# Linear attention and two MLPs on one core: two operand sums change engine, the next x operands change time, four results change buffer

## The chip, the cores and the metric

One core of one Trainium2 chip runs the whole program. The metric is device time in microseconds (us), the median of several executions; lower is better. One more execution was recorded by the hardware profiler, and every duration below is from that one. Engines are called as the profile calls them: PE is TensorE (its weight loads are PEld), DVE is VectorE, ACT is ScalarE, POOL is GpSimd, SP is the queue of SyncE, which issues nearly all DMAs.

## The reference

```python
q_s = softmax(q, over the head dimension);  k_s = softmax(k, over the sequence)
kv = einsum('bhsd,bhse->bhde', k_s, v);     attn = einsum('bhsd,bhde->bhse', q_s, kv)
x = attn as (4608 tokens, 512)
h = x @ w_in;   x = (h * clip(h + 3, 0, 6) / 6) @ w_out        # first MLP, 512 -> 2048 -> 512
h = x @ w2_in;  out = (h * sigmoid(h)) @ w2_out                # second MLP, same sizes
```

Everything is float32.

## The kernel before

**Number format.** PE multiplies in fp32r, a shorter float32. Each operand is split into a rounded upper part (ACT, a cast) and the rest, the lower part (DVE, a subtraction); a product takes three matmuls, upper by upper, upper by lower and lower by upper.

**First MLP (phase 0).** Tokens go in 9 blocks of 512 (j = 0 to 8) with 16 steps f of 128 hidden units each. A step is `mm1` (L486, 12 matmuls), `gate` (L543) and `mm2` (L552, 12 matmuls into four PSUM banks y0 to y3). After the 16th step `finish` (L567) scales the four banks by 1/6 into tiles `o` and stores them to `yd` in DRAM; DVE takes the even ones, ACT the odd ones. The tiles come from the pool `tmp`, tag `t2k`, which has six buffers and serves most short-lived tiles of the kernel. In the same phase the second MLP's weights are converted, summed and stored to `ws` (class `Parts`, L173); the tile they are stored from has the tag `sp` (one buffer). A tile of tag `qT` (one buffer) serves the attention.

**Second MLP (`second_mlp`, L961).** Blocks 1 to 8 are taken in four pairs (b = 0 to 3). For each pair the two products are done by a scheme that needs seven products P1 to P7 of half-size blocks instead of eight, with sums of blocks as operands and sums of the results afterwards. Block 0 is done last, in the plain way. One pair has two stages, both cut into slots of six matmuls (128x512):

- The inner stage, the first product: 8 groups n of seven slots (`inner`, L983). Behind each group come sums on DVE and one on POOL, sigmoids on ACT, multiplications on DVE that leave the gated values in four half tiles of g (`pair_events`, L1010), and on POOL `t1` and `t2` (L1048, L1051), which make two more operands of the second product: T1, in place, and T2, in the tile `spare`.
- The outer stage, the second product: seven products in the order P1, P5, P6, P2, P7, P3, P4, eight slots i each (`outer`, L1137). Before each slot its operand is split, upper on ACT (`split`, L1079) and lower on DVE (`split_low`, L1083), into one of five tile pairs taken in turn (`split_tile`, L1066). P7 and P4 need two more sums: `next_t3(i)` (L1087) overwrites g1[:, 0], which P1 has used, with T3, and `next_t4(i)` (L1091) overwrites g1[:, 1], which P5 has used, with T4. Both run on POOL. `joins` (L1151) adds the results.

During the inner stages of pairs 0 to 2, `x_ahead` (L1096) makes the operands of the pair after: twice (c = 0 and 1) it loads four tiles from `yd`, makes four sums on POOL (`total`), splits seven operands (`high` on ACT L1109, `low` on DVE L1113) and stores fourteen tiles to `xd`. The outer stage then fetches those (`x_fetch`). The weights arrive through a ring of six buffers (`fetch`, L876).

**Order.** Nothing is reordered by a compiler: every engine works through its own queue in program order. In the second MLP that order is a list of events, `when(t, fn)`, sorted by t, and t is counted in slots: a pair begins at t0, `start[0] = t0 + 55` is the first outer slot, and an event at t stands between the matmuls of slot t and the next. LOOK = 4 puts a split about four slots ahead of its matmuls:

```python
when(t - LOOK + 0.2, lambda b=b, p=p, i=i: split(b, p, i))
when(t - LOOK + 0.5, lambda b=b, p=p, i=i: split_low(b, p, i))
```

The last step of the first MLP is placed at `when(1.95, ...)`, behind the first two slots of pair 0: `mm2(last)` and `finish(0, 8)`.

Of the kernel before, what the change touches and what calls it, by code (L numbers as in the profile page):

```python
# [9 lines left out]
F32 = mybir.dt.float32  # L10
F32R = mybir.dt.float32r
AF = mybir.ActivationFunctionType
ALU = mybir.AluOpType
# [5 lines left out]
P = 128  # L19
# [4 lines left out]
def f32(ap):  # L24
    return ap.bitcast(F32)
# [3 lines left out]
def efficient_attention_then_two_mlps(  # L29
# [11 lines left out]
    nc = tc.nc  # L41
# [6 lines left out]
    NB = NT // BLK  # L48
# [9 lines left out]
    tmp = ctx.enter_context(tc.tile_pool(name="tmp", bufs=6))  # L58
    raw = ctx.enter_context(tc.tile_pool(name="raw", bufs=2))
    gs = ctx.enter_context(tc.tile_pool(name="gs", bufs=2))  # L60
    att = ctx.enter_context(tc.tile_pool(name="att", bufs=1))
# [100 lines left out]
    def slot(o, i, part):  # L162
        if part == "A21":
            return 7 * NPR + i
        if o:
            return OUTER.index(part) * NPR + i
        if part == "A22":
            return 6 + 7 * i + 2 if i < NPR - 1 else 7 * NPR - 1
        return (0 if i == 0 else 6 + 7 * (i - 1)) + INNER.index(part) + (
            1 if i and part not in INNER[:2] else 0  # L170
        )
# [394 lines left out]

    def finish(ph, j):  # L567
        for c, y in enumerate(acc.pop((ph, j))):
            o = tmp.tile([P, 512], F32, tag="t2k", name="o")
            if ph == 0:  # L570
                if c % 2:
                    nc.scalar.mul(o, y, 1.0 / 6.0)
                else:
                    nc.vector.tensor_scalar_mul(o, y, 1.0 / 6.0)
                nc.sync.dma_start(yd[j, c], o)
            else:
                (nc.scalar.copy if c % 2 else nc.vector.tensor_copy)(o, y)
                rows = out[j * BLK : (j + 1) * BLK, :].rearrange("(p i) d -> i p d", i=NCH)
                nc.sync.dma_start(rows[c], o)
# [37 lines left out]
    for i, u in enumerate(range(2, NP)):  # L617
        o = i * (KB + VB + QB)
# [240 lines left out]
    ring, op, gw, ev = [], {}, {}, []  # L859
    LOOK = 4  # L860

    def when(t, fn):
        ev.append((t, len(ev), fn))
# [97 lines left out]
    def second_mlp(last):  # L961
# [16 lines left out]
        def add(out, a, b, how=ALU.add, eng=None):  # L978
            (eng or nc.vector).tensor_tensor(out=out, in0=a, in1=b, op=how)  # L979
# [18 lines left out]
        def g_of(f):  # L998
            if f not in gw:
                gw[f] = wts.tile([P, 2, BLK], F32, tag="wo", name="g2")  # L1000
            return gw[f]
# [64 lines left out]
        def split_tile(x=False):  # L1066
            n = 2 + turns[0] % 3 if x else turns[0] % 5
            turns[0] += 1
            if n == 4:
                return [  # L1070
                    att.tile([P, BLK], F32R, tag=tag, bufs=1, name="gsp") for tag in ("ke", "qe")
                ]
            if n < 2:
                t = gs.tile([P, 2, BLK], F32R, tag="g", name="gsp")
            else:
                t = att.tile([P, 2, BLK], F32R, tag=("sp", "qT")[n - 2], bufs=1, name="gsp")
            return [t[:, 0], t[:, 1]]

        def split(b, p, i):  # L1079
            t = d["sp", b, p, i] = split_tile()  # L1080
            nc.scalar.copy(t[0], source(p, i))  # L1081

        def split_low(b, p, i):  # L1083
            t = d["sp", b, p, i]
            add(t[1], source(p, i), f32(t[0]), ALU.subtract)

        def next_t3(i):  # L1087
            g1 = g_of(2 * i)
            add(g1[:, 0], op["spare"][:, i], g1[:, 0], ALU.subtract, nc.gpsimd)

        def next_t4(i):  # L1091
            add(g_of(2 * i)[:, 1], g_of(2 * i + 1)[:, 0], op["spare"][:, i], ALU.subtract, nc.gpsimd)

        XS = ("B11", "T2", "T1", "B21", "T3", "B22", "T4")

        def x_ahead(j, c, t, step):  # L1096

            st, hl = {}, {}

            def load(n):  # L1100
                if n in ("B22", "B21"):
                    pair = gs.tile([P, 2, BLK], F32, tag="g", name="xst")
                    st[n], st[{"B22": "B12", "B21": "B11"}[n]] = pair[:, 0], pair[:, 1]
                jj, h = j + (n[2] == "2"), int(n[1] == "2")
                nc.sync.dma_start(st[n], yd[jj, 2 * h + c])

            def high(n, src):
                hl[n] = split_tile(True)
                nc.scalar.copy(hl[n][0], st[src])  # L1109

            def low(n, src):
                hi, lo = hl.pop(n)
                add(lo, st[src], f32(hi), ALU.subtract)  # L1113
                to = xd[XS.index(n)]
                nc.sync.dma_start(to[:, 0, c], f32(hi))
                nc.sync.dma_start(to[:, 1, c], f32(lo))

            def total(to, x, y):
                add(st[to], st[x], st[y], ALU.subtract, nc.gpsimd)

            for m, n in enumerate(("B22", "B12", "B21", "B11")):
                when(t - 4.0 + 0.3 * m, lambda n=n: load(n))
            for m, (n, src) in enumerate((
                ("B22", "B22"), ("B21", "B21"), ("T1", "B12"), ("T2", "B22"), ("B11", "B11"),
                ("T4", "B21"), ("T3", "B11"),
            )):
                when(t + m * step + 0.3, lambda n=n, src=src: high(n, src))
                when(t + m * step + 0.9, lambda n=n, src=src: low(n, src))
            when(t + 0.02, lambda: total("B12", "B12", "B11"))
            when(t + 1 * step + 0.25, lambda: total("B22", "B22", "B12"))  # L1130
            when(t + 3 * step + 0.25, lambda: total("B21", "B21", "B22"))
            when(t + 4 * step + 1.0, lambda: total("B11", "B22", "B11"))
# [63 lines left out]
        for b in range(BB):  # L1196
            t0 = T
            place = {}
            for n in range(NPR):
                at = place[n] = {}  # L1200
                for p in ("P1", "P6"):
                    at[p], T = T, T + 1
                if n:
                    place[n - 1]["P4"], T = T, T + 1
                for p in ("P5", "P2", "P7", "P3"):
                    at[p], T = T, T + 1
            t2 = T
            start = {}
            for u in range(7 * NPR):
                start[u], T = T, T + 1  # L1210
                if u == 0:
                    place[NPR - 1]["P4"], T = T, T + 1
            for n in range(NPR):
                pair_events(b, n, place[n])
                for p, t in place[n].items():
                    k = 7 * NPR * b + slot(0, n, PAIR[p][0]) // 2
                    uses[k] = max(uses.get(k, 0.0), t)
            for u in range(7 * NPR):
                p, i = KEYS[u // NPR], u % NPR
                t = start[u]  # L1220
                when(t - LOOK + 0.2, lambda b=b, p=p, i=i: split(b, p, i))
                when(t - LOOK + 0.5, lambda b=b, p=p, i=i: split_low(b, p, i))
                if p == "P1":
                    when(start[0] + 6.4 + 3.0 * i, lambda i=i: next_t3(i))
                if p == "P6":
                    when(start[0] + 26.4 + 2.8 * i, lambda i=i: next_t4(i))
                when(t, lambda b=b, p=p, i=i: outer(b, p, i))
                k = 7 * NPR * b + 7 * NPR // 2 + u // 2
                uses[k] = max(uses.get(k, 0.0), t)
                if i == NPR - 1:  # L1230
                    joins(b, p, t + 1.3)
            j = 1 + 2 * b
            if b + 1 < BB:
                x_ahead(j + 2, 0, t0 + 9.0, 3.2)
                x_ahead(j + 2, 1, t0 + 31.0, 3.2)
                for m, n in enumerate(XS):
                    for low in range(2):
                        when(
                            start[0] + 3.1 + 6.0 * m + 3.0 * low,
                            lambda n=n, low=low: x_fetch(n, low),  # L1240
                        )
                for k in range(2 * NCH):
                    when(T + 3.95 + 5.0 * k, lambda j=j, k=k: turn(j, k))
            else:
                def begin_last():
                    op.pop("spare")
                base = start[0]
                for c in range(NC):
                    when(base + 44.3 + c, lambda c=c: load_y(0, c))
                    when(base + 48.4 + 2 * c, lambda c=c: split_y(0, c))  # L1250
                for f in range(NF):
                    when(base + (4.2 + 2.2 * f if f < 14 else 100.0), lambda f=f: load_split(f, 0))
                for f in range(0, NF, 2):
                    when(base + 48.3 + 0.5 * f, lambda f=f: load_split(f, 1))
# [24 lines left out]
    with tc.manual_schedule(engines=None):  # L1279
# [34 lines left out]
        for n, s in list(enumerate(steps))[NF:]:  # L1314
            ph, j, f = s
# [123 lines left out]
```

## Time and profile before

| | us |
|---|---|
| median of 3 runs (lowest, highest) | 1645.51 (1644.49, 1646.26) |
| the profiled execution | 1645.06 |
| its span, first to last instruction | 1643.3 |
| PE / DVE / ACT / POOL busy in the span | 1611.2 / 1082.1 / 748.6 / 422.4 |
| second MLP, four pairs | from about 899 to 1548 |

The profile's time is split by engine, by line and by stretch. Instructions that run through the helper `add` (L978) all carry line 979, so they are told apart by the names of their tiles: `gsp` is a split tile, `g` a gated tile, `xst` a loaded x tile, `pb` a PSUM bank. A timeline row gives start, length, engine, line, operation and tiles, a count where rows of one kind are merged, and in brackets the idle time of the engine just before and what ended it.

### The profile page before, as it was taken

To read this page: it belongs to the slowest core of one execution; us is meant where nothing else is said; L and a number is where in the kernel's file an instruction comes from. 1 tells how busy PE (TensorE), PEld (TensorE's weight loads), DVE (VectorE), ACT (ScalarE), POOL (GpSimd) and SP (SyncE) were. 2 spreads that over 40 slices of the span, in tenths; PEclk is the share of its full clock that TensorE was granted. 3 is DMA by queue.
4 is the path that set the end of the run, shared out by engine and by line. 5 is a ranking of instruction groups with operands and counts; after the bars stand their busy time and mean duration, and the time that the engine had idled before them with its cause. 6 is when DMAs were issued, how large, how long until landed. Compare 5 with 4: busy or idle time off the path is not lost.

```text
span 1643.3 us, 21988 instructions
## 1 busy us (share of the span) xinstructions
PE 1611.2 (98%) x7612; PEld 1301.1 (79%) x7612; DVE 1082.1 (66%) x1721; ACT 748.6 (46%) x1322; POOL 422.4 (26%) x334
## 2 busy tenths in 40 slices
PE   6999999999999999999999999999999999999998
PEld 4777888888888888888888787887788878887887
DVE  8996666666666666655555689567956885578522
ACT  6885444444434444443434454344435543444322
POOL 2100111111111111111121456055705560345000
PEclk9999999999999999999999999999999999999999
DMA  9912435454543445343341998798879986669730
GB/s 270 325 35 68 133 107 141 124 151 119 170 136 110 140 120 151 110 135 103 113 157 58 334 327 298 250 316 307 301 254 314 342 291 246 216 226 330 251 128 26
DMA packets 291838, 317.61 MB, mean 193 GB/s; under 512 B 113424, under 2 KB 197392, under 8 KB 291728
## 3 DMA queue, kind: packets, MB, share of 16 engines
q1 hardware_dynamic: 228768, 300.97, 54.5%
q10 hardware_dynamic: 62960, 15.25, 4.1%
q8 instruction: 60, 0.98, 0.2%
q14 instruction: 50, 0.41, 0.1%
HBM read 234.62 MB, written 81.53 MB: 192 GB/s over the span
## 4 chain that ended last, share of the span: by engine, by line
PE 84%; DVE 11%; DMA 2%; ACT 2%; issue 1%; POOL 1%; SPq 0%; ACTq 0%; DVEq 0%; POOLq 0%
PE h L493 25%; PE y L563 22%; PE pb L992 16%; PE pb L1145 13%; DVE gsp L979 5%; PE y L565 3%; PE pa L451 2%; PE pa L337 1%; DVE fa L132 1%; DVE fa L128 1%; PE pb L1185 1%; DMA ring<-ws 1%; DMA xd<-gsp 0%; DMA xst<-yd 0%; DVE fa L121 0%
## 5 line engine op out<-in xcount | busy, mean ns | idle before, releaser
L493 PE MATMUL h<-x,wi 128*128 128x512 f32 x1920 | 472.6, 394 | 2.3 <-DVE wi L153 1.0
L493 PEld LDWEIGHTS h<-x,wi 128*128 128x128 f32 x1920 | 356.5, 188 | 78.7 <-DVE wi L153 2.4
L563 PE MATMUL y<-g,wo 128*128 128x512 f32 x1728 | 418.1, 391 | 0.0
L563 PEld LDWEIGHTS y<-g,wo 128*128 128x128 f32 x1728 | 322.4, 188 | 68.1
L1145 PE MATMUL pb<-gsp,ring 128*128 128x512 f32 x1344 | 321.2, 395 | 1.9
L992 PE MATMUL pb<-xo,ring 128*128 128x512 f32 x1344 | 315.5, 393 | 5.3 <-ACT s L1023 3.0
L1145 PEld LDWEIGHTS pb<-gsp,ring 128*128 128x128 f32 x1344 | 248.9, 188 | 73.2 <-DVE gsp L979 23.2
L992 PEld LDWEIGHTS pb<-xo,ring 128*128 128x128 f32 x1344 | 250.7, 188 | 58.6 <-ACT s L1023 3.4
L513 DVE SCALAR_TENSOR_TENSOR r<-r,h 128x512 f32<-128x512 f32 x128 | 87.8, 686 | 198.5 <-ACT r L506 198.3
L979 DVE TENSOR_TENSOR gsp<-g,gsp 128x512 fp32r<-128x512 f32 x192 | 174.4, 928 | 61.5 <-ACT gsp L1081 58.2
L1081 ACT CAST gsp<-g 128x512 fp32r<-128x512 f32 x192 | 117.6, 622 | 123.1 <-DVE gsp L979 68.1
L506 ACT ACTIVATE r<-h 128x512 f32<-128x512 f32 x144 | 86.2, 599 | 145.7 <-PE h L493 126.1
L521 ACT CAST g<-r 128x512 fp32r<-128x512 f32 x144 | 89.5, 622 | 119.9 <-DVE r L513 107.8
L524 DVE TENSOR_TENSOR g<-r,g 128x512 fp32r<-128x512 f32 x144 | 103.9, 721 | 53.6 <-ACT g L521 43.8
L398 POOL TENSOR_TENSOR qe<-qe,qs 128x512 f32<-128x512 f32 x36 | 37.7, 1046 | 347.4 <-DVE qs L393 292.4
L979 POOL TENSOR_TENSOR s<-U,s 128x512 f32<-128x512 f32 x32 | 45.1, 1408 | 262.1 <-DVE U L979 238.9
L979 DVE TENSOR_TENSOR g<-r,pb 128x512 f32<-128x512 f32 x96 | 65.6, 683 | 51.1 <-ACT r L1005 50.9
L376 POOL TENSOR_TENSOR qe<-qraw,qm 128x512 f32<-128x512 f32 x34 | 36.0, 1058 | 208.2 <-DVE qm L368 132.7
L1005 ACT ACTIVATE r<-pb 128x512 f32<-128x512 f32 x96 | 57.2, 596 | 62.0 <-DVE pb L979 49.2
L197 POOL TENSOR_TENSOR ws_sum<-fa 128x256 f32<-128x256 f32 x32 | 29.5, 921 | 156.0 <-ACT r L506 88.5
L354 ACT ACTIVATE kv<-pa,rs 64x64 fp32r<-64x64 f32 x56 | 17.3, 309 | 109.7 <-DMA qt<-zd 55.2
L979 POOL TENSOR_TENSOR g<-g 128x512 f32<-128x512 f32 x32 | 42.9, 1341 | 64.4 <-DVE g L979 64.4
(155 smaller groups left out, 1688.9 us busy)
## 6 DMA issues: line engine op xcount, KB each, us to landing
ring<-ws SPq DMA_DIRECT2D x224, 512.0 KB, 4.8
ws<-sp SPq DMA_DIRECT2D x128, 256.0 KB, 2.5
xd<-gsp SPq DMA_DIRECT2D x84, 256.0 KB, 6.1
xo<-xd SPq DMA_DIRECT2D x42, 512.0 KB, 5.4
yd<-o SPq DMA_DIRECT2D x36, 256.0 KB, 2.7
wi_early<-in_moe_w_in_dram SPq DMA_DIRECT2D x16, 512.0 KB, 9.0
wo_early<-in_moe_w_out_dram SPq DMA_DIRECT2D x16, 512.0 KB, 9.4
wi_raw<-in_moe_w_in_dram SPq DMA_DIRECT2D x16, 512.0 KB, 4.4
```

What stands on the lines that cost most here:

```text
L493: nc.tensor.matmul(h, w[:, a, c, :], x[:, e, c, :], start=(c == 0 and n == 0), stop=(c == NC - 1 and n == 2),)
L506: nc.scalar.activation(self.r, self.h, AF.Relu, bias=3.0)
L513: nc.vector.scalar_tensor_tensor(out=r, in0=r, scalar=6.0, in1=h, op0=ALU.min, op1=ALU.mult)
L521: nc.scalar.copy(self.g[:, 0], self.r)
L524: nc.vector.tensor_tensor(out=self.g[:, 1], in0=self.r, in1=f32(self.g[:, 0]), op=ALU.subtract)
L563: nc.tensor.matmul(y[c], w[:, a, cs], g[:, e, :], start=st, stop=sp)
L565: nc.tensor.matmul(y[c], g[:, e, cs], w[:, a, :], start=st, stop=sp)
L979: (eng or nc.vector).tensor_tensor(out=out, in0=a, in1=b, op=how)
L992: nc.tensor.matmul(to, ws_[:, a], e[:, c], start=p in ("P1", "P6", "P5") and c == 0 and m == 0, stop=c == 1 and m == 2, skip_group_check=True,
L1005: nc.scalar.activation(r, d[b, n, key], AF.Sigmoid)
L1081: nc.scalar.copy(t[0], source(p, i))
L1145: nc.tensor.matmul(d[b, p][m], w[:, a, m * P : (m + 1) * P], t[e], start=new and i == 0 and k == 0, stop=i == NPR - 1 and k == 2, skip_gro ...
```

## The change

`finish` takes its four tiles for block 8 from two tiles of two halves, of the tags `sp` and `qT`, and no longer from `t2k`. `next_t3` and `next_t4` run on DVE (the default of `add`), at other event times. The two runs of `x_ahead` begin 2 and 3 slots earlier, with 3.0 slots between operands where there were 3.2.

```diff
--- before.py
+++ after.py
@@ -566,7 +566,13 @@
 
     def finish(ph, j):
         for c, y in enumerate(acc.pop((ph, j))):
-            o = tmp.tile([P, 512], F32, tag="t2k", name="o")
+            if j < NB - 1:
+                o = tmp.tile([P, 512], F32, tag="t2k", name="o")
+            elif c % 2 == 0:
+                pair = att.tile([P, 2, 512], F32, tag=("sp", "qT")[c // 2], bufs=1, name="o")
+                o = pair[:, 0]
+            else:
+                o = pair[:, 1]
             if ph == 0:
                 if c % 2:
                     nc.scalar.mul(o, y, 1.0 / 6.0)
@@ -1086,10 +1092,10 @@
 
         def next_t3(i):
             g1 = g_of(2 * i)
-            add(g1[:, 0], op["spare"][:, i], g1[:, 0], ALU.subtract, nc.gpsimd)
+            add(g1[:, 0], op["spare"][:, i], g1[:, 0], ALU.subtract)
 
         def next_t4(i):
-            add(g_of(2 * i)[:, 1], g_of(2 * i + 1)[:, 0], op["spare"][:, i], ALU.subtract, nc.gpsimd)
+            add(g_of(2 * i)[:, 1], g_of(2 * i + 1)[:, 0], op["spare"][:, i], ALU.subtract)
 
         XS = ("B11", "T2", "T1", "B21", "T3", "B22", "T4")
 
@@ -1221,9 +1227,9 @@
                 when(t - LOOK + 0.2, lambda b=b, p=p, i=i: split(b, p, i))
                 when(t - LOOK + 0.5, lambda b=b, p=p, i=i: split_low(b, p, i))
                 if p == "P1":
-                    when(start[0] + 6.4 + 3.0 * i, lambda i=i: next_t3(i))
+                    when(start[0] + 8.7 + 2.6 * i, lambda i=i: next_t3(i))
                 if p == "P6":
-                    when(start[0] + 26.4 + 2.8 * i, lambda i=i: next_t4(i))
+                    when(start[0] + 29.7 + 2.2 * i, lambda i=i: next_t4(i))
                 when(t, lambda b=b, p=p, i=i: outer(b, p, i))
                 k = 7 * NPR * b + 7 * NPR // 2 + u // 2
                 uses[k] = max(uses.get(k, 0.0), t)
@@ -1231,8 +1237,8 @@
                     joins(b, p, t + 1.3)
             j = 1 + 2 * b
             if b + 1 < BB:
-                x_ahead(j + 2, 0, t0 + 9.0, 3.2)
-                x_ahead(j + 2, 1, t0 + 31.0, 3.2)
+                x_ahead(j + 2, 0, t0 + 7.0, 3.0)
+                x_ahead(j + 2, 1, t0 + 28.0, 3.0)
                 for m, n in enumerate(XS):
                     for low in range(2):
                         when(
```

## Rows read from the trace of the kernel before

**Rows 1.** The page, part 1: busy time and share of each engine.

```profile
PE 1611.2 (98%) x7612; PEld 1301.1 (79%) x7612; DVE 1082.1 (66%) x1721; ACT 748.6 (46%) x1322; POOL 422.4 (26%) x334
```

**Rows 2.** Waits of PEld, 900 to 1560 us: total us, times, longest.

```profile
PEld pb L1145 <- DVE gsp L979: 23.2, 51, 0.5
PEld pb L992 <- ACT s L1023: 3.4, 1, 3.4
PEld pb L992 <- DVE U L979: 3.0, 2, 2.7
```

**Rows 3.** Chain that ended last: start, length, what (merged pieces).

```profile
909.74 7.32 DMA xst<-yd
...
1174.83 1.66 PE pb L1145 x6
...
1176.53 1.66 PE pb L1145 x6
...
1226.24 5.44 PE pb L992 x24
```

**Rows 4.** Timeline of DVE in the outer stage of pair 1.

```profile
1151.51 16.48 DVE L979 TENSOR_TENSOR gsp<-g,gsp 128x512 fp32r<-128x512 f32 x10
...
1203.81 0.69 DVE L979 TENSOR_TENSOR gsp<-g,gsp 128x512 fp32r<-128x512 f32 x1 [0.67 <-ACT gsp L1081]
1204.42 0.68 DVE L979 TENSOR_TENSOR U<-pb,kbuf 128x512 f32<-128x512 f32 x1
```

**Rows 5.** Timeline of POOL, end of pair 1's inner stage and its outer stage.

```profile
1134.07 1.29 POOL L979 TENSOR_TENSOR g<-g 128x512 f32<-128x512 f32 x1 [2.07 <-DVE g L979]
...
1152.11 11.94 POOL L979 TENSOR_TENSOR g<-spare,g 128x512 f32<-128x512 f32 x7
...
1167.39 11.93 POOL L979 TENSOR_TENSOR g<-g,spare 128x512 f32<-128x512 f32 x7
```

**Rows 6.** Groups by line: busy us, mean ns, idle before.

```profile
L979 POOL TENSOR_TENSOR g<-spare,g 128x512 f32<-128x512 f32 x32 | 54.7, 1739 | 0.0
L979 POOL TENSOR_TENSOR g<-g,spare 128x512 f32<-128x512 f32 x32 | 54.6, 1737 | 0.0
```

**Rows 7.** Timelines around the start of pair 0 (PE, ACT, DVE, SP).

```profile
904.75 8.32 PE L992 MATMUL pb<-xo,ring 128*128 128x512 f32 x36
915.36 4.95 PE L992 MATMUL pb<-xo,ring 128*128 128x512 f32 x19 [2.29 <-DVE U L979]
...
912.09 1.28 ACT L1005 ACT_TABLE_LOAD   x1 [5.19 <-DMA yd<-o]
...
914.62 0.68 DVE L979 TENSOR_TENSOR U<-pb,s 128x512 f32<-128x512 f32 x1
...
909.74 3.05 SPq L1105 DMA_DIRECT2D xst<-yd  x4
```

**Rows 8.** Timelines around the end of pair 1's inner stage (PE, ACT, DVE, SP).

```profile
1142.06 2.63 PE L992 MATMUL pb<-xo,ring 128*128 128x512 f32 x6 [3.01 <-ACT s L1023]
1144.49 2.18 PE L1145 MATMUL pb<-gsp,ring 128*128 128x512 f32 x6
1146.51 1.55 PE L992 MATMUL pb<-xo,ring 128*128 128x512 f32 x6
...
1140.42 0.62 ACT L1081 CAST gsp<-g 128x512 fp32r<-128x512 f32 x1 [6.27 <-DMA xd<-gsp]
...
1135.62 1.66 DVE L979 TENSOR_TENSOR gsp<-xst,gsp 128x512 fp32r<-128x512 f32 x1
...
1137.30 0.33 SPq L1116 DMA_DIRECT2D xd<-gsp  x1
```

**Rows 9.** Stretches: us, busy of PE, PEld, DVE, ACT, POOL; PEclk, DMA, GB/s.

```profile
1139.00:1180.00 41.00, 37.60 (x147) 27.62 (x146) 38.09 (x32) 20.84 (x37) 32.11 (x19) 0.96 0.73 255
...
1144.00:1226.00 82.00, 81.61 (x344) 64.15 (x343) 63.27 (x70) 36.60 (x62) 32.11 (x19) 0.99 0.76 268
1226.00:1305.00 79.00, 79.00 (x365) 65.22 (x364) 53.52 (x76) 37.72 (x70) 40.09 (x29) 1.00 0.94 324
```

## The prediction

> **What bounds the kernel now.** I read the page first: PE is busy in 98% of the span, DVE in 66%, POOL in 26% [rows 1]. So the kernel is PE-bound as a whole, and only the places where PE waits can be won. Matmuls are pipelined and a waiting one can still look busy, so I took the waits from the weight loads, from 900 us on, where the second MLP runs. Three entries matter [rows 2]: 51 waits on DVE's lower parts of the split tiles, 23.2 us in sum and none over 0.5 us; one wait of 3.4 us on an ACT copy; two on a DVE sum, 3.0 us. A wait of PEld is partly slack, because the load has a matmul to hide behind, so 23.2 us is a ceiling. The real price shows in the chain: undisturbed, 24 matmuls take 5.44 us, 0.2267 each and 1.36 us for a slot of six; in the slow part of an outer stage slots start 1.70 us apart (1174.83, 1176.53) [rows 3]. A slow slot loses 0.34 us, and 51 of them 17.3 us.
>
> Why DVE is late there: in pair 1 its lower parts take 1.65 us each from 1151.5 on (16.48 us for ten), and 0.69 us later in the same stage, where DVE is idle 0.67 us before such a row [rows 4]. What differs is POOL: from 1152.11 to 1179.3 it runs the sixteen `next_t3` and `next_t4` with no pause (11.94 and 11.93 us for seven), and from there on nothing [rows 5]. Their event times lie 3.0 and 2.8 slots apart, but POOL has nothing else in its queue and what they wait for comes early, so they run as one block. Each of the two engines slows the other: POOL needs 1.74 us for a sum [rows 6], against 1.29 us for one of the same shape that meets less DVE work [rows 5].
>
> **The change, part by part, against the profiled execution (1645.06 us, 0.45 below the median shown).**
>
> 1. *T3 and T4 to DVE.* 64 POOL operations (54.7 + 54.6 us) go [rows 6], and with them DVE's 1.65 us; 64 DVE operations come. Neither sum was on the path by itself; POOL's time was paid only through DVE. What is won is the 51 slow slots: **17.3 us**. For their price I take the lower part, a subtraction of the same shape with two SBUF inputs: 0.69 us alone, and what is queued behind it starts 0.61 us later (1203.81, 1204.42) [rows 4]. I take 0.69; the ends are 0.61 and the slowed 1.65. Cover: a slot lasts 1.36 us and a lower part takes 0.69, so 0.67 us per slot is free. `next_t3` adds one per 2.6 slots (0.27 us a slot), `next_t4` one per 2.2 slots (0.31 us). Where `joins` also puts one sum in each slot, the queued costs are 0.61 + 0.61 + 0.31 = 1.53 against 1.36: 0.17 us too much over four slots, 0.7 us, which the lead of four slots (5.4 us) takes. Nothing of the 64 falls on the path by this count. No wait is added on DVE: P1 and P5 have used the overwritten halves slots before, `t2` has written `spare` long before, and P7 and P4 read the results from slots 32 and 48 on, while the sums end near 27 and 45.
>
> The Trainium skill, page "SBUF — State Buffer", section "Who interferes with whom", says that a VectorE instruction with two SBUF inputs and a GpSimd instruction that reads SBUF lock each other out, and that the loser "fully blocks". By that a pair would take 0.69 + 1.29 = 1.98 us and a slow slot lose 0.62, 31.6 us in all. The rows give 1.70 us for the pair, so the two overlap in part, and the sum above goes by the rows.
>
> 2. *Results of block 8 in `sp` and `qT`.* At the start of pair 0 PE runs 36 matmuls from 904.75, which at 0.2267 end at 912.91; the next starts at 915.36 [rows 7]: 2.45 us lost. Backwards: that matmul waits for a DVE sum (U, 914.62), which stands behind a multiplication that needs the first sigmoid, and ACT's table load ahead of that sigmoid waited 5.19 us until 912.09 for a store `yd<-o` to land [rows 7]: the sigmoid's result tile is the seventh of six `t2k` buffers after four `o`. With `o` elsewhere it starts when P2 is done, near 907.5, and U3 follows some two to three us later, ahead of 912.9. Gain **2.45 us**. What comes next: the first x operand now stands 2 slots earlier, and its lower part on DVE is queued at 7.9, ahead of the sum U2 of the next group (8.1), which P7 of that group needs at slot 11, near 917.0. In this trace the x tile was issued at 909.74, landed 7.32 us later [rows 3], behind rings and results; one ring of 0.5 MB fewer stands before it now, 1.6 us at the 324 GB/s of a busy stage [rows 9]: landed near 915.5, cast 916.1, lower part 916.8, U2 917.4. That costs **0.5 us** (0 to 2: up to that if it lands as late as now).
>
> 3. *x operands earlier.* Per pair 0 to 2 this moves 8 loads, 28 stores, 14 casts, 14 lower parts and 8 POOL sums, by 2 slots at the first and 4.2 at the last. All of it lies in inner stages, where PE ran at full speed throughout in pair 2 (79.00 busy of 79.00, DVE 53.5, ACT 37.7, POOL 40.1) [rows 9]; the rate of work rises by 3.2 / 3.0 only. On SP it is moved past one or two ring fetches; the ring holds six, twelve slots of work. The one place on the path is in pair 1: the last lower part ran from 1135.62, 1.66 us, its store was issued at 1137.30, and ACT sat 6.27 us until 1140.42 for it to release the tile of the first outer split [rows 8]. The copy `s5`, queued behind, came late and PE stood 3.01 us; then its matmuls came 0.43 us apart instead of 0.23, with a mean granted clock of 0.96 in that stretch [rows 8, 9] (full speed is 2.4 GHz, and twice the spacing fits the 1.2 GHz level): six in 2.43 us (1142.06 to 1144.49) and six in 2.02, against 1.36: 1.07 + 0.66 more [rows 8]. Ended 4.2 slots (5.7 us) earlier, ACT's wait falls from 6.27 to about 0.6 us, less than the 3.3 us that it could lose before PE felt it. Gain **4.7 us** (0 if SP brings the store no sooner).
>
> Sum: 17.3 + 2.45 - 0.5 + 4.7 = 24.0 us; 1645.06 - 24.0 = 1621.1, and 0.45 more against the median: **1621.5 us**.
>
> **Rivals.**
> - *Full gain* (0.65): as above, 1619 to 1623.5 by the bounds of 2.
> - *The two small waits stay* (0.18): a new wait on x at the start of pair 0 (2 us) and pair 1's wait for the store, because SP issues in order and the DMA share is 0.94 in such a stage [rows 9]. Then only the slow slots go, and perhaps 1 us more: about 1627.
> - *Half of the slow slots stay* (0.11): sums and joins on DVE eat the lead and half the 17.3 us remains: 1630. Against it: the lower parts wait for ACT, not for DVE, once POOL is quiet [rows 4].
> - *Slower: the sums are on the path* (0.03). `next_t3` and `next_t4` stand in front of lower parts in one queue. If DVE has no lead at those slots, each delays PE by what it takes queued, 0.61 us: 64 x 0.61 = 39.0, less 24.0 won: 1660. It decides where DVE's work per slot passes 1.36 us over a long stretch; at 0.69 + 0.31 it does not, at 1.1 us a split it would. DVE's total speaks against it: 63.27 us in 70 operations now in an outer stage of 82 us [rows 9], 86 x 0.69 = 59.3 us of 77.6 then. The Trainium skill, page "VectorE: DVE Perf Modes", section "The DRAIN you can't avoid", says that the next operation can't issue before the pipe is empty; by that each sum costs 0.69 and this case 64 x 0.69 - 24.0 = 20.2 us, 1665. The rows show starts 0.61 us apart, so I keep 0.61.
> - *The change does not do what it says* (0.03): something else than POOL, a DMA or ACT, makes DVE slow, and it stays at 1.65 us: within 0.2% of now, 1641 to 1646. Against it: the slow time ends with POOL's last sum, 1179.3, in the same stage.
>
> **How the numbers follow.** 0.2% is 3.3 us, about what a measurement of this kernel can tell from no change. The first three cases are all faster by more: 0.94. The last gives 0.03 for no difference, the fourth 0.03 for slower. The range takes the first case whole, with 1 us for the spread of the runs below it, and the second with 2 us above it, and most of the third stays out: 1618 to 1629.
>
> **What would show it right.** In outer stages lower parts of 0.69 us after the first few slots, and no spacing of 1.70 us; an outer stage of 77.6 us instead of 82; the 64 sums on DVE at about 0.69 us; POOL about 109 us less busy; no ACT wait on `yd<-o` ahead of the first sigmoid, and PE without a gap at 915; ACT's wait for `xd<-gsp` under 1 us in pair 1 and no gap of PE at 1139. Wrong would be: PEld still waiting for `gsp` some 50 times, or new waits of PE on `U` or `s` in the inner stages.

## The result, and the profile after

The changed kernel takes **1623.5 us** (median of 4 runs, 1622.82 to 1624.02) against 1645.27 us for the kernel before in the same session (4 runs): a ratio of 0.9867, 95% interval 0.985 to 0.9884, 21.8 us less. Forecast were 1621.5 us and 1618 to 1629. The profiled execution took 1623.47 us with a span of 1621.5 us. Six lines are new ahead of the second MLP, so L979 of before is L985 here, L992 is L998, L1145 is L1151, L1081 is L1087.

The page, part 1, against [rows 1]: POOL is 108.1 us less busy, DVE 27.2 us less although it does 64 instructions more, and PE busy falls by 17.9 us with as many matmuls, since a waiting matmul counts as busy.

```profile
PE 1593.3 (98%) x7612; PEld 1302.4 (80%) x7612; DVE 1054.9 (65%) x1785; ACT 747.9 (46%) x1322; POOL 314.3 (19%) x270
```

The waits of PEld from 890 to 1560 us, against [rows 2]. The 51 waits on `gsp` are gone; what is left names a DVE sum and two kinds of ACT copy, and all of it lies before 980 us, in pair 0's inner stage:

```profile
PEld pb L998 <- DVE U L985: 1.7, 1, 1.7
PEld pb L998 <- ACT s L1029: 1.1, 3, 0.5
PEld pb L998 <- ACT s L1023: 0.9, 2, 0.5
```

The groups by line, against [rows 6]. The sums cost 0.69 us each on DVE, where they took 1.74 on POOL, and the lower parts from `spare`, which took 1.64 us on average beside POOL before, are back at 0.69 us (the first line is from the kernel before):

```profile
L979 DVE TENSOR_TENSOR gsp<-spare,gsp 128x512 fp32r<-128x512 f32 x32 | 50.3, 1638 | 0.0
...
L985 DVE TENSOR_TENSOR gsp<-spare,gsp 128x512 fp32r<-128x512 f32 x32 | 22.1, 692 | 14.1 <-ACT gsp L1087 13.3
...
L985 DVE TENSOR_TENSOR g<-spare,g 128x512 f32<-128x512 f32 x32 | 21.9, 686 | 0.0
L985 DVE TENSOR_TENSOR g<-g,spare 128x512 f32<-128x512 f32 x32 | 21.9, 684 | 0.0
```

The timeline of DVE in the outer stage of pair 1, against [rows 4]. A sum starts 0.61 us after the lower part ahead of it and ends before the next one's upper part is there; between sums DVE still has its 0.67 us of idle time:

```profile
1147.56 0.69 DVE L985 TENSOR_TENSOR gsp<-g,gsp 128x512 fp32r<-128x512 f32 x1 [0.67 <-ACT gsp L1087]
1148.17 0.69 DVE L985 TENSOR_TENSOR g<-spare,g 128x512 f32<-128x512 f32 x1
1148.92 0.69 DVE L985 TENSOR_TENSOR gsp<-g,gsp 128x512 fp32r<-128x512 f32 x1
1150.28 0.69 DVE L985 TENSOR_TENSOR gsp<-g,gsp 128x512 fp32r<-128x512 f32 x1 [0.67 <-ACT gsp L1087]
```

The timeline of PE from the start of pair 0 to the end of pair 1. It gives the lengths of stages: an outer stage lasts from the first `gsp` matmul to the first long run of `xo` matmuls behind it, 1057.05 - 979.53 = 77.52 us and 1213.35 - 1135.83 = 77.52, an inner stage 1135.83 - 1057.05 = 78.78:

```profile
899.11 2.88 PE L998 MATMUL pb<-xo,ring 128*128 128x512 f32 x12
901.83 2.88 PE L563 MATMUL y<-g,wo 128*128 128x512 f32 x12
904.55 12.40 PE L998 MATMUL pb<-xo,ring 128*128 128x512 f32 x54
918.18 61.51 PE L998 MATMUL pb<-xo,ring 128*128 128x512 f32 x264 [1.23 <-DVE U L985]
979.53 1.52 PE L1151 MATMUL pb<-gsp,ring 128*128 128x512 f32 x6
...
1057.05 5.61 PE L998 MATMUL pb<-xo,ring 128*128 128x512 f32 x24
...
1135.83 1.52 PE L1151 MATMUL pb<-gsp,ring 128*128 128x512 f32 x6
...
1213.35 5.61 PE L998 MATMUL pb<-xo,ring 128*128 128x512 f32 x24
```

Read in this way from each trace (us; pair 3 has no x operands; the last line of the table belongs to runs below):

| stage | before | after | sums only | x only | results only | after, old x times in pair 0 |
|---|---|---|---|---|---|---|
| pair 0 inner | 80.5 | 80.4 | 80.0 | 81.6 | 77.9 | 77.8 |
| pair 0 outer | 81.7 | 77.5 | 77.5 | 81.7 | 81.7 | 77.5 |
| pair 1 inner | 83.0 | 78.8 | 82.0 | 79.0 | 83.0 | 79.7 |
| pair 1 outer | 81.6 | 77.5 | 77.8 | 81.7 | 81.9 | 77.5 |
| pair 2 inner | 78.8 | 78.8 | 78.9 | 79.0 | 78.8 | 78.8 |
| pair 2 outer | 82.4 | 77.5 | 77.7 | 81.7 | 82.2 | 77.5 |
| pair 3 inner | 78.8 | 78.8 | 78.8 | 78.8 | 78.8 | 78.8 |
| pair 3 outer | 81.7 | 77.5 | 77.5 | 81.7 | 81.7 | 77.5 |
| median of the runs | 1645.3 | 1623.5 | 1627.1 | 1641.4 | 1642.8 | 1621.8, 1622.1 |

So of the 21.6 us that the eight stages lost, 17.3 came from the four outer stages, 4.2 from pair 1's inner stage, and nothing from pair 0's, where 2 us had been forecast. An outer stage of 342 matmuls at 0.2267 us is 77.5 us: no wait is left there.

**Pair 0's inner stage** kept its length with other waits. ACT's table load follows the copy ahead of it with no wait for a store, against [rows 7] (timelines of ACT, DVE and SP around the start):

```profile
906.72 1.28 ACT L1011 ACT_TABLE_LOAD   x1
908.01 0.60 ACT L1011 ACTIVATE r<-pb 128x512 f32<-128x512 f32 x1
...
916.19 0.62 ACT L1115 CAST gsp<-xst 128x512 fp32r<-128x512 f32 x1 [3.11 <-DMA xst<-yd]
...
916.84 0.69 DVE L985 TENSOR_TENSOR gsp<-xst,gsp 128x512 fp32r<-128x512 f32 x1 [3.40 <-ACT gsp L1115]
917.45 0.68 DVE L985 TENSOR_TENSOR U<-pb,s 128x512 f32<-128x512 f32 x1
...
908.50 4.11 SPq L1111 DMA_DIRECT2D xst<-yd  x4
```

The gap at 915 us is gone. But ACT now waits 3.11 us for the first x tile, the lower part follows at 916.84, U2 stands behind it at 917.45, and PE, which had done 54 matmuls by 904.55 + 54 x 0.2267 = 916.79, goes on at 918.18: 1.39 us lost. The stage is 80.42 - 342 x 0.2267 = 2.89 us above its matmuls; the other 1.5 us lie in later and smaller waits, five of them of 0.1 to 0.3 us for ACT's copies (1.2 us).

**The end of pair 1's inner stage**, against [rows 8]: ACT waits 0.88 us where it had waited 6.27, and PE passes from one stage to the next without a gap (timelines of ACT and PE):

```profile
1130.76 0.62 ACT L1087 CAST gsp<-g 128x512 fp32r<-128x512 f32 x1 [0.88 <-DMA xd<-gsp]
...
1129.71 6.28 PE L998 MATMUL pb<-xo,ring 128*128 128x512 f32 x27
```

### The profile page after: what moved, and what is told of

It reads as the page before. It is cut to its first block, busy times and chain, and to the rows that moved or that the text cites. A ratio compares the mean times of both kernels' runs of the same rounds, so it can differ in the third digit from the quotient of the medians.

```text
span 1621.5 us, 22000 instructions
## 1 busy us (share of the span) xinstructions
PE 1593.3 (98%) x7612; PEld 1302.4 (80%) x7612; DVE 1054.9 (65%) x1785; ACT 747.9 (46%) x1322; POOL 314.3 (19%) x270
## 4 chain that ended last, share of the span: by engine, by line
PE 90%; DVE 5%; DMA 2%; ACT 1%; issue 1%; POOL 0%; SPq 0%; ACTq 0%; DVEq 0%; POOLq 0%
PE h L493 25%; PE y L563 22%; PE pb L1151 19%; PE pb L998 18%; PE y L565 3%; PE pa L451 2%; PE pa L337 1%; DVE fa L132 1%; DVE fa L128 1%; PE pb L1191 1%; DMA yd<-o 0%; DVE fa L121 0%; DVE wi L153 0%; DMA ring<-ws 0%; DMA ws<-sp 0%
## 5 line engine op out<-in xcount | busy, mean ns | idle before, releaser
L998 PE MATMUL pb<-xo,ring 128*128 128x512 f32 x1344 | 315.0, 392 | 1.3 <-DVE U L985 1.2
L1151 PE MATMUL pb<-gsp,ring 128*128 128x512 f32 x1344 | 305.9, 389 | 0.0
L1151 PEld LDWEIGHTS pb<-gsp,ring 128*128 128x128 f32 x1344 | 252.3, 188 | 52.3
L998 PEld LDWEIGHTS pb<-xo,ring 128*128 128x128 f32 x1344 | 250.1, 188 | 55.0 <-DVE U L985 1.7
L985 DVE TENSOR_TENSOR gsp<-g,gsp 128x512 fp32r<-128x512 f32 x192 | 138.1, 725 | 55.0 <-ACT gsp L1087 51.4
L1087 ACT CAST gsp<-g 128x512 fp32r<-128x512 f32 x192 | 117.6, 623 | 106.5 <-DVE gsp L985 76.7
L985 POOL TENSOR_TENSOR s<-U,s 128x512 f32<-128x512 f32 x32 | 45.4, 1419 | 324.1 <-DVE U L985 323.1
L985 DVE TENSOR_TENSOR g<-r,pb 128x512 f32<-128x512 f32 x96 | 65.5, 682 | 41.9 <-ACT r L1011 41.9
L354 ACT ACTIVATE kv<-pa,rs 64x64 fp32r<-64x64 f32 x56 | 17.3, 308 | 108.2 <-DMA qt<-zd 57.2
L1011 ACT ACTIVATE r<-s 128x512 f32<-128x512 f32 x32 | 20.2, 633 | 81.4 <-POOL s L985 81.4
```

The costliest lines, as they stand in the source:

```text
L998: nc.tensor.matmul(to, ws_[:, a], e[:, c], start=p in ("P1", "P6", "P5") and c == 0 and m == 0, stop=c == 1 and m == 2, skip_group_check=True,
L1011: nc.scalar.activation(r, d[b, n, key], AF.Sigmoid)
L1151: nc.tensor.matmul(d[b, p][m], w[:, a, m * P : (m + 1) * P], t[e], start=new and i == 0 and k == 0, stop=i == NPR - 1 and k == 2, skip_gro ...
```

## The experiments

**1. Sums only.** The kernel before, with this alone:

```diff
-            add(g1[:, 0], op["spare"][:, i], g1[:, 0], ALU.subtract, nc.gpsimd)
+            add(g1[:, 0], op["spare"][:, i], g1[:, 0], ALU.subtract)
...
-                    when(start[0] + 6.4 + 3.0 * i, lambda i=i: next_t3(i))
+                    when(start[0] + 8.7 + 2.6 * i, lambda i=i: next_t3(i))
```

and the same for T4.

> The kernel before with T3 and T4 on VectorE at the new event times, and nothing else of the change. Theory (GpSimd's block of sums slows VectorE): all four outer stages fall from 81.6 to 82.4 us to 77.5, the inner stages stay (80.5, 83.0, 78.8, 78.8); 1645.3 - 17.3 = 1628.0 us. Rival (VectorE enters the outer stages late because of the x operands): outer stages stay above 81 us, the time within 2 us of 1645.

Measured: 1627.07 us (1626.61 to 1627.55), ratio 0.9893 (0.9878 to 0.9907), 17.6 us less than 1644.68 on that chip. The outer stages are 77.5 to 77.8 us, also in pair 3, which no x operand precedes. The theory holds and the rival falls. Pair 1's inner stage keeps its wait, 2.89 us (82.0 us).

**2. x operands only.** The kernel before, with this alone:

```diff
-                x_ahead(j + 2, 0, t0 + 9.0, 3.2)
-                x_ahead(j + 2, 1, t0 + 31.0, 3.2)
+                x_ahead(j + 2, 0, t0 + 7.0, 3.0)
+                x_ahead(j + 2, 1, t0 + 28.0, 3.0)
```

> The kernel before with the x operands at the new event times, and nothing else of the change. Theory: the inner stage of pair 1 falls from 83.0 to 78.8 us, its outer stage loses the 0.7 us at the lower clock, the other outer stages stay at 81.7 to 82.4; at the start of pair 0 nothing won or up to 2 us lost: 1639 to 1642.5 us. Rival (x operands make VectorE late in the outer stages): these fall to near 78 us where x operands stood before them (pairs 0 to 2), about 1629 us.

Measured: 1641.44 us, ratio 0.9979 (0.9969 to 0.9988), 3.2 us less. Pair 1's inner stage falls to 79.0 us, the outer stages stay at 81.7, PEld's waits on `gsp` are 52 with 23.5 us. The x operands win nothing in outer stages, not even the 0.7 us that were expected in pair 1's: its first slots are no longer slow, but PEld waits for `gsp` 13 times there as in the three others, where it had waited 10 times before. In pair 0 they lose 1.1 us (81.6 us): behind the old gap a second wait on the sum U has come (timeline of PE at the start of pair 0):

```profile
905.49 8.32 PE L992 MATMUL pb<-xo,ring 128*128 128x512 f32 x36
915.73 4.72 PE L992 MATMUL pb<-xo,ring 128*128 128x512 f32 x18 [1.93 <-DVE U L979]
920.85 60.93 PE L992 MATMUL pb<-xo,ring 128*128 128x512 f32 x264 [0.40 <-DVE U L979]
```

**3. Results only.** The kernel before, with the tiles of `finish` alone:

```diff
-            o = tmp.tile([P, 512], F32, tag="t2k", name="o")
+            if j < NB - 1:
+                o = tmp.tile([P, 512], F32, tag="t2k", name="o")
+            elif c % 2 == 0:
+                pair = att.tile([P, 2, 512], F32, tag=("sp", "qT")[c // 2], bufs=1, name="o")
+                o = pair[:, 0]
+            else:
+                o = pair[:, 1]
```

> The kernel before with the results of block 8 in their own tiles, and nothing else of the change. Theory: the first sigmoid no longer waits for a store, the gap of 2.45 us at 915 us goes, the inner stage of pair 0 falls from 80.5 to about 78.0 us and the rest stays: 1642.8 us. Rival (the start is short of DMA bandwidth, and the next late load takes the gap over): pair 0's inner stage stays at 80 us or more, 1645 us.

Measured: 1642.80 us, ratio 0.9988 (0.9979 to 0.9997), 1.9 us less, with 0.5 to 3.5 us inside the interval. Pair 0's inner stage is 77.9 us, 2.6 us shorter, and PE runs it without a gap:

```profile
905.37 72.63 PE L998 MATMUL pb<-xo,ring 128*128 128x512 f32 x318
977.84 1.52 PE L1151 MATMUL pb<-gsp,ring 128*128 128x512 f32 x6
```

So in its stage this part alone wins what was forecast for it, 2.45 us, and no late load takes the gap over: the rival falls. In the whole change something takes it back.

**4. The change, with the old x times in pair 0.** In the changed kernel:

```diff
-                x_ahead(j + 2, 0, t0 + 7.0, 3.0)
-                x_ahead(j + 2, 1, t0 + 28.0, 3.0)
+                x_ahead(j + 2, 0, t0 + (7.0 if b else 9.0), 3.0 if b else 3.2)
+                x_ahead(j + 2, 1, t0 + (28.0 if b else 31.0), 3.0 if b else 3.2)
```

> The changed kernel, but with the old event times of the x operands in pair 0 alone. Theory (in pair 0 the earlier x operands took what the results' own tiles won, because a lower part that waits for its load stands ahead of U2 in VectorE's queue): pair 0's inner stage falls from 80.4 to between 78.0 and 78.7 us, the other stages stay at 77.5 and 78.8; 1621 to 1622 us. Rival (the start is short of DMA bandwidth whatever the order): it stays at 80 us or more, 1623.5 us.

Measured: 1621.80 us (1621.47 to 1622.46), pair 0's inner stage 77.8 us. It was run again beside the changed kernel on one chip:

> The changed kernel once more, beside the next one on the same chip: 1623.5 us, outer stages 77.5 us each, inner stages 80.4, 78.8, 78.8, 78.8.

> The changed kernel with the old event times of the x operands in pair 0, once more. Theory: 1.7 us under the changed kernel, 1621.8 us, pair 0's inner stage 77.8 us. Rival (the first run's difference was between chips): no difference beyond 0.5 us.

Measured: 1623.68 us (1623.15 to 1624.59) for the changed kernel and 1622.11 us (1621.85 to 1622.58) for this one; pair 0's inner stage is 80.6 against 78.5 us. All four runs of the one lie under all four of the other, by 1.6 us in the median; the ratios to the kernel before, 0.987 (0.9855 to 0.9885) and 0.986 (0.9844 to 0.9877), overlap, so the difference rests on the two sets of runs on one chip. This is the best version found. That the earlier x operands take back pair 0's gain is shown: the stage follows them in both directions (runs 2 and 4).

**5. Sums on VectorE at the old times.** In the changed kernel:

```diff
-                    when(start[0] + 8.7 + 2.6 * i, lambda i=i: next_t3(i))
+                    when(start[0] + 6.4 + 3.0 * i, lambda i=i: next_t3(i))
...
-                    when(start[0] + 29.7 + 2.2 * i, lambda i=i: next_t4(i))
+                    when(start[0] + 26.4 + 2.8 * i, lambda i=i: next_t4(i))
```

> The changed kernel with T3 and T4 on VectorE at their old event times (6.4 + 3.0 i and 26.4 + 2.8 i). Theory (the engine matters, not the times: VectorE has 0.67 us free in each slot): outer stages stay at 77.5 us, 1623.5 us. Rival (the new spacing is needed to keep VectorE's lead): outer stages of 78.5 us or more, 1627 us or more.

Measured: one run, 1624.24 us, all four outer stages 77.5 us. The new spacing is not needed. On POOL the event times spread nothing: its queue held nothing else, what the sums read was there, and it ran them without a pause [rows 5]. On DVE the queue itself spreads them, by the lower parts in between (timeline of DVE in pair 1's outer stage):

```profile
1149.00 0.69 DVE L985 TENSOR_TENSOR g<-spare,g 128x512 f32<-128x512 f32 x1
1149.75 0.69 DVE L985 TENSOR_TENSOR gsp<-g,gsp 128x512 fp32r<-128x512 f32 x1
...
1153.08 0.69 DVE L985 TENSOR_TENSOR g<-spare,g 128x512 f32<-128x512 f32 x1
```

**6. GpSimd only writes.** The kernel before, with zeros written in place of T3 and T4 (these two operands are left out):

```diff
-            add(g1[:, 0], op["spare"][:, i], g1[:, 0], ALU.subtract, nc.gpsimd)
+            nc.gpsimd.memset(g1[:, 0], 0.0)
...
-            add(g_of(2 * i)[:, 1], g_of(2 * i + 1)[:, 0], op["spare"][:, i], ALU.subtract, nc.gpsimd)
+            nc.gpsimd.memset(g_of(2 * i)[:, 1], 0.0)
```

> The kernel before, with the 64 sums T3 and T4 on GpSimd replaced by as many writes of zero to the same halves: T3 and T4 are left out, GpSimd writes and reads nothing. Theory (GpSimd's reads of SBUF and VectorE's second input get in each other's way): VectorE's lower parts beside the writes take 0.69 us, outer stages 77.5 us, 1628 us. Rival (any work of GpSimd on SBUF slows VectorE): lower parts beside the writes take over 1 us; the outer stages then lose in proportion to how long the writes last.

Measured: one run, 1627.86 us; outer stages 77.5, 77.8, 77.5, 77.5 us. The timelines of DVE and POOL in pair 1's outer stage show lower parts of 0.69 us that overlap writes of 0.53 us; in the whole trace 26 lower parts run beside such writes alone, and the longest takes 0.70 us:

```profile
1150.50 0.69 DVE L979 TENSOR_TENSOR gsp<-g,gsp 128x512 fp32r<-128x512 f32 x1 [0.61 <-ACT gsp L1081]
1151.86 0.69 DVE L979 TENSOR_TENSOR gsp<-g,gsp 128x512 fp32r<-128x512 f32 x1 [0.67 <-ACT gsp L1081]
...
1150.37 0.53 POOL L1092 MEMSET g<- 128x512 f32 x1
1150.84 0.53 POOL L1089 MEMSET g<- 128x512 f32 x1
1151.31 1.00 POOL L1092 MEMSET g<- 128x512 f32 x2
```

So it is not GpSimd's work as such that slows VectorE: the sums, which read SBUF, do, and writes of zero do not. The Trainium skill says this on its page "SBUF — State Buffer", section "Who interferes with whom": VectorE with two SBUF inputs contends with a GpSimd instruction that reads SBUF, "not with one that only writes it". This trace agrees, 0.69 us beside writes and 1.65 beside reads [rows 4]. A write of zeros differs from a sum in its length too (0.53 us against 1.74), but lower parts that overlap one are not slowed at all.

**7. x operands of pair 0 later still.** In the changed kernel:

```diff
-                x_ahead(j + 2, 0, t0 + 7.0, 3.0)
-                x_ahead(j + 2, 1, t0 + 28.0, 3.0)
+                x_ahead(j + 2, 0, t0 + (7.0 if b else 11.0), 3.0)
+                x_ahead(j + 2, 1, t0 + (28.0 if b else 32.0), 3.0)
```

> The changed kernel with the x operands of pair 0 later still, at 11.0 and 32.0 (step 3.0); pairs 1 and 2 as changed. Theory (in pair 0 each wait comes from an x load that lands after its place in the queues): pair 0's inner stage 77.6 to 78.2 us, 1621.5 us, as with the old times or a little better. Rival (what was won at the start now returns at the end of the stage, where the last stores release the first split's tile): inner stage of pair 0 over 79 us.

Measured: 1623.14 us (1621.80 to 1623.59), pair 0's inner stage 79.6 us. The theory fails; the stage is as long as the rival said, but not for its reason. No wait is left at 918 us, but small ones stand at 927 to 929 and 955 to 959 us, not at the end, where the rival put them. Later is not better without end: the x work then delays other work. In this trace a POOL sum of x from 951.15 to 952.44 us stands ahead of the sum `s`, and the sigmoid at 953.73 waits 3.99 us for that. On another chip than the changed kernel, and with runs that reach from 1621.80 to 1623.59, the time itself shows no difference from it.

**8. The first lower part behind U2.** In the changed kernel:

```diff
-                when(t + m * step + 0.9, lambda n=n, src=src: low(n, src))
+                when(t + m * step + (0.9 if m else 1.5), lambda n=n, src=src: low(n, src))
```

> The changed kernel with one thing exchanged: the first lower part of each run of x operands stands behind U2 in VectorE's queue (1.5 slots after the run's start instead of 0.9). Theory: the gap of 1.2 us at 918 us goes, pair 0's inner stage falls by 1.0 to 1.4 us to about 79.1, and the smaller waits on ACT copies (1.2 us) stay: 1622.3 us. Rival (PE waits there for ACT, held up by the load, and not for VectorE's order): inner stage of 80.0 us or more, 1623.5 us.

Measured: 1622.56 us (1622.00 to 1623.02), pair 0's inner stage 79.7 us. PE's wait for U is gone, but the load is as late as before, and the next in line takes over: the ACT copy `s5` (L1029). The timelines of PE, ACT and DVE show its way: the lower part at 916.87, held up by the load, still stands ahead of another DVE sum (`pb`, 917.48), the sigmoid at 918.20 waits 1.36 us for that sum, and `s5` stands behind the sigmoid.

```profile
904.92 13.76 PE L998 MATMUL pb<-xo,ring 128*128 128x512 f32 x60
919.33 7.10 PE L998 MATMUL pb<-xo,ring 128*128 128x512 f32 x30 [0.65 <-ACT s L1029]
926.99 52.31 PE L998 MATMUL pb<-xo,ring 128*128 128x512 f32 x228 [0.56 <-ACT s L1023]
...
916.22 0.62 ACT L1115 CAST gsp<-xst 128x512 fp32r<-128x512 f32 x1 [2.76 <-DMA xst<-yd]
918.20 0.60 ACT L1011 ACTIVATE r<-pb 128x512 f32<-128x512 f32 x1 [1.36 <-DVE pb L985]
918.70 0.58 ACT L1029 COPY s<-pb 128x512 f32<-128x512 f32 x1
...
916.87 0.69 DVE L985 TENSOR_TENSOR gsp<-xst,gsp 128x512 fp32r<-128x512 f32 x1 [2.46 <-ACT gsp L1115]
917.48 0.69 DVE L985 TENSOR_TENSOR pb<-s,pb 128x512 f32<-128x512 f32 x1
```

The stage is 0.8 us shorter than the changed kernel's, where 1.0 to 1.4 were expected; two executions of one kernel differ by as much as 0.7 us here, so the size is not certain. The order in DVE's queue explains the first wait and, one sum later, the next: a late load holds up whatever stands behind its lower part.

## Why the prediction was right

- **Which waits bound it.** Right: the 51 slow slots were all there was to win in the outer stages. Forecast 17.3 us; the four outer stages fell by 17.3 us, of which 0.7 belong to the lower clock at the start of pair 1's (part 3 of the prediction), so 16.7 us are the slow slots, 0.33 us for each of the 51 where 0.34 was taken. Run 1 shows that moving the sums does it alone, and run 6 what in the sums did the harm.
- **The sums on DVE cost nothing.** Right: 0.69 us each, started 0.61 us behind a lower part, no `gsp` wait left. The rival with the sums on the path needed a lower part of 1.1 us; it takes 0.69. Run 5 shows that the old spacing does as well. The Trainium skill, page "VectorE: DVE Perf Modes", section "The DRAIN you can't avoid", says that the next operation waits until the pipe is empty, and adds that one which is not held starts earlier, which the prediction left out. This trace agrees with what it adds: starts 0.61 us apart with operations of 0.69. As the sums lie in idle time, the time would not tell the two apart.
- **x operands in pair 1.** Right: forecast 4.7 us, measured 4.2 in the inner stage and 0.7 in the outer. ACT's wait fell to 0.88 us (forecast 0.6).
- **Results in their own tiles.** The mechanism was right and its gain too: forecast 2.45 us, alone it won 2.6 (run 3).
- **The step that was mis-sized** is the cost set against it: "That costs **0.5 us** (0 to 2: up to that if it lands as late as now)". The gap at U2 was placed rightly, but it took 1.39 us: the x tile landed 0.6 us later than worked out (at 916.09 by the trace, 7.59 us after its issue; worked out were 915.5), and the slot that needs U2 came at 916.79, 0.2 us earlier. With a ring fewer ahead of it the load had been put 1.6 us earlier than before; it landed 1.0 us earlier. And it was not the only one: small waits on ACT copies came behind it, some 1.2 us more. One of them, at 956 us in the changed kernel's timelines (POOL first, then ACT), shows the way: a POOL sum of x stands ahead of the sum `s`, the sigmoid waits for that, and the copy that PE needs is last in the row.

```profile
951.39 1.28 POOL L985 TENSOR_TENSOR xst<-xst 128x512 f32<-128x512 f32 x1
952.64 1.73 POOL L985 TENSOR_TENSOR s<-U,s 128x512 f32<-128x512 f32 x1
...
954.41 0.63 ACT L1011 ACTIVATE r<-s 128x512 f32<-128x512 f32 x1 [4.30 <-POOL s L985]
954.94 0.58 ACT L1011 ACTIVATE r<-pb 128x512 f32<-128x512 f32 x1
955.42 0.58 ACT L1023 COPY s<-pb 128x512 f32<-128x512 f32 x1
```

  In all, the earlier x operands cost 2.1 to 2.6 us there (80.6 against 78.5 and 80.4 against 77.8, run 4), above the bound given, so pair 0's inner stage won 0.06 us where 1.95 were forecast. That is nearly the whole difference between 24.0 and 21.8 us. It is the first half of the rival in which the two small waits stay, and the sign "new waits of PE on `U` or `s` in the inner stages", which the prediction had named as showing it wrong, came in this one stage. The cost was bounded by one wait that was found; the waits behind it were not looked for.

What stays open: pair 0's inner stage differs by up to 0.7 us between executions of one kernel (77.8 and 78.5 in run 4's kernel; 80.4 and 80.6 in the changed one), so which of its small waits each kernel has is not settled below that. With the changed x times in pairs 1 and 2 the inner stage of pair 1 had 0.5 to 0.9 us of such waits in some executions (79.3 in the second profile of the changed kernel, 79.7 in run 4).

## What to carry to other kernels

An operation that is cheap for its own engine can be dear for another: where VectorE's operations take twice their usual time, look what GpSimd does in the same stretch, and whether it reads SBUF. Event times in this program spread work only on an engine whose queue holds other work; an engine with nothing else to do runs its jobs as a block, once what they read is there. And a load that is moved earlier in the list of events has to be followed through every in-order queue that it can block, not only to the first wait: three parts that win 17.6, 3.2 and 1.9 us alone won 21.8 together, because one took back, at one place, what another had won.

## What was not expected of the hardware

- VectorE and GpSimd both slow down beside each other, but a pair of operations takes 1.70 us, less than 0.69 + 1.29 = 1.98 us one after the other [rows 3, 5]. The Trainium skill's "fully blocks", on the page "SBUF — State Buffer" (for two SBUF inputs it stands in the section "SBUF: two separate sides"), is stricter than what these rows show.
- A wait of PE of 2.9 to 3.3 us at the same place was followed by matmuls 0.43 us apart, the clock's lower level of 1.2 GHz, in three kernels (before 3.01 us, results only 3.31, GpSimd writing 2.89) but not in the one with the sums only, where the six matmuls behind a wait of 2.89 us took 1.51 us (in the kernel before 2.43). The granted clock is the last but two of the columns, in the 5 us in which the wait ends (kernel before, then GpSimd writing, then sums only; the waits end at 1142.06, 1137.07 and 1137.72):

```profile
1141.00:1146.00 5.00, 3.94 (x10) 3.12 (x11) 4.24 (x7) 3.05 (x7) 0.93 (x1) 0.66 0.33 121
```

```profile
1136.00:1141.00 5.00, 3.93 (x10) 3.13 (x11) 4.23 (x7) 3.06 (x7) 0.92 (x1) 0.66 0.38 138
```

```profile
1136.00:1141.00 5.00, 3.27 (x14) 2.47 (x14) 3.57 (x6) 3.64 (x7) 0.26 (x1) 1.00 0.48 172
```

Why the clock fell behind one wait of 2.89 us and not behind the other isn't shown.
